# Clustered attention with two MLPs on one core: the centroid similarities with the centroids as stationary operand in four column tiles

## The chip, the core and the metric

The kernel runs on one core of a Trainium2 chip. The metric is the time of one execution on the device, in microseconds (us). The engines are named as the profile names them: PE is TensorE's matmul, PEld its weight load, DVE is VectorE, ACT is ScalarE, POOL is GpSimd, SP is SyncE, which only issues DMAs here.

## What is computed

For 16 heads (2 batches of 8) of 768 tokens by 64 features, each query and key is assigned to the nearest of 16 centroids of its head. A query attends only to keys with the same centroid. The result, laid out as 1536 tokens by 512 features, goes through two MLPs.

```python
q_assign = np.argmax(np.einsum('bhsd,hcd->bhsc', q_n, c_n), axis=-1)
k_assign = np.argmax(np.einsum('bhsd,hcd->bhsc', k_n, c_n), axis=-1)
mask = q_assign[:, :, :, None] == k_assign[:, :, None, :]
scores = scale * np.matmul(q, k.transpose(0, 1, 3, 2))
scores = np.where(mask, scores, -1000000000.0)
...
h = np.maximum(np.maximum(x @ w1, x @ w2), x @ w3)
return (h @ w_out).astype(np.float32)
```

## The kernel before

Two heads make a pair; there are eight pairs, p = 0 to 7, and `qT` and `kT` hold a pair as 128 features by 768 tokens. A unit is 256 queries of one head: 48 units, six to a pair. For a unit the kernel computes scores of 128 queries by 768 keys twice (`scores`, S0 and S1, tile s), the negated row maximum on DVE (`maxima`, M0 and M1, tile mx), the exponential on ACT (`exps`, X0 and X1, tile ee), transposes of it on PE by an identity (`transposes`, T0, T2 and T4, four matmuls each, tile t), copies out of PSUM split into two rounded parts eh and el (E on ACT, L on DVE or POOL), and products with the values (`values`, V0, V2 and V4, four matmuls each, tile o). The mask is carried by extra rows of the score operands: rows 64 to 79 of q2 are the query's one-hot centroid, those of k2 hold 0 or a large negative number.

The order of everything in the attention is written out by hand. `ORDER` has six strings, one for each unit of a pair; "S0/-2" stands for S0 of the unit two ahead, "G0+2" for the operation on the pair two ahead. Each engine executes its part of this list in the list's order. One walk through the six strings is called a turn here, and its strings units 0 to 5. `BEGIN` and `END` hold the first and last operations; the sims of pairs 0 and 1 stand in `BEGIN`.

The change touches the way from a pair's raw operands to the one-hot rows, all of it for a pair that is scored later:

- G0 and G1 (`sims`, line 417): six matmuls each, with 128 tokens of q (G0) or k (G1) as weights and the pair's 32 centroid columns `cb` (block-diagonal over the two heads) as moving operand. They write the spare 256 columns of a score tile, beside its 768 columns of scores.
- N0a, N0b, N1a, N1b (`near_max`, `near_eq`, lines 429 and 435): on DVE, the maximum over the 16 centroids and the equality with it, for q and for k.
- W, FA, FB (lines 447 to 472): the first of equal maxima is kept; the one-hot tile oh of 128 tokens by 6 x 64 comes out in bf16.
- O0 and O1 (`onehot_T`, line 474): three transposes each of 128 tokens by 64 one-hot columns, bf16, into 64 rows of PSUM, again in a score tile's spare columns.
- P0 and P1 (`penalties`, line 492): ACT scales and shifts 64 x 384 of them into the tile oo.
- D0 and D1 (`operands`, line 500): SP issues the DMAs that put the operands together, among them two of 16 x 768 from oo for each head.

G0 stands in unit 2, G1 in unit 3, O0 and P0 in unit 0, O1 and P1 in unit 1. PSUM has eight banks: two score tiles of two banks each (pool `ps_s`), three of one bank for the transposes (pool `ps_t`, tag t) and one for o. A buffer of `ps_t` is given to the next tile that asks for one as soon as the last reader of its old tile stands in the list, and the new writer waits for that reader.

Of the kernel before, what the change touches and what calls it, by code (L numbers as in the profile page):

```python
# [8 lines left out]
F32 = mybir.dt.float32  # L9
F32R = mybir.dt.float32r  # L10
BF16 = mybir.dt.bfloat16
AF = mybir.ActivationFunctionType
ALU = mybir.AluOpType
AX = mybir.AxisListType
# [3 lines left out]
P = 128  # L18
B, H, S, D = 2, 8, 768, 64
C = 16  # L20
NP = H // 2
NPAIR = B * NP
NQ = S // P
G = 256
# [10 lines left out]
SCALE = 0.125  # L35
BIG = 2.0**100
ORDER = (
# [25 lines left out]
)  # L63

ONCE = {
# [10 lines left out]
ENGINE = {"QH": "A", "QH@1": "P", "KH": "P", "VH": "P", "KL": "P", "KL@0": "D", "VL": "P", "W": "P", "W@1": "D"}  # L76
WARM = (8, 4)
PACE = 0.16
FIRST = ("G0", "G1", "N0a", "N0b", "N1a", "N1b", "W", "QH", "KH", "QL", "LD")
SPARE = {"G0": (4, 0), "G1": (5, 0), "O0": (2, 0), "O1": (3, 0)}  # L80
WP = 512

W_LEAST = 2.0 ** ((896 >> 3) - 127)
# [4 lines left out]
def clustered_attention_mlps(  # L88
# [16 lines left out]
    nc = tc.nc  # L105
    PSUM = bass.MemoryType.PSUM

    const = ctx.enter_context(tc.tile_pool(name="const", bufs=1))
# [104 lines left out]
    mlp, m = ctx.enter_context(ExitStack()), {}  # L213
# [104 lines left out]
    with ExitStack() as att:  # L318
# [8 lines left out]
        sm = pool(att, "sm", 2, side="right")  # L327
        ps_t = pool(att, "ps_t", 3, PSUM, "right")
# [10 lines left out]
        idf = const.tile([P, P], F32, name="idf")  # L339
        idb = const.tile([P, P], BF16, name="idb")  # L340
        desc = const.tile([P, C], F32, name="desc")
        gain = const.tile([D + C, 1], F32, name="gain")
        base = const.tile([D + C, 1], F32, name="base")
        cb = const.tile([P, NP, 2 * C], F32, name="cb")


# [2 lines left out]
        st = {}  # L349
# [50 lines left out]
        def split_v(p, part):  # L400
            s = st[p]
            if part == 0:

                s["vs"] = vp.tile([P, NQ, 4, D], F32R, tag="vs", name=f"vs{p}")
            hi, lo = s["vs"][:, :, 0:4:3, :], s["vs"][:, :, 1:3, :]
            if part == 0:
                rounded(engine("VH", p), hi, s["rv"])
            else:
                rest(engine("VL", p), lo, s["rv"], hi)
# [74 lines left out]
        def onehot_up(p, j, ps):  # L484
            ps = ps.bitcast(BF16)[0 : D + C, 0:S]
            for t in range(NQ):
# [2 lines left out]
                    ps[:, t * P : (t + 1) * P], st[p]["oh"][:, c - C : c + D], idb  # L489
                )  # L490

        def penalties(p, half, spare, engine="A"):
            ps = spare.bitcast(BF16)[0 : 4 * C, 0 : S // 2]
            oo = st[p]["oo"][:, half * S // 2 : (half + 1) * S // 2]
            if engine == "A":
                nc.scalar.activation(oo, ps, AF.Identity, scale=gain[0 : 4 * C], bias=base[0 : 4 * C])  # L496
            else:
                nc.vector.tensor_scalar(oo, ps, gain[0 : 4 * C], base[0 : 4 * C], op0=ALU.mult, op1=ALU.add)

        def operands(p, part, heads=(0, 1), queue=nc.sync):  # L500
            s = st[p]

            def dma(out, in_):
                queue.dma_start(out=out.bitcast(F32), in_=in_.bitcast(F32))

            for j in heads:
                r = slice(j * D, (j + 1) * D)
                if part == 0:
                    q1 = opn.tile([P, S], F32R, tag="q1", name=f"q1_{p}_{j}")
                    q2 = opn.tile([D + C, S], F32R, tag="q2", name=f"q2_{p}_{j}")  # L510
                    k1 = opn.tile([P, S], F32R, tag="k1", name=f"k1_{p}_{j}")
                    k2 = opn.tile([D + C, S], F32R, tag="k2", name=f"k2_{p}_{j}")
                    s[j] = (q1, q2, k1, k2)
                    dma(q1[0:D], s["qh"][r])
                    dma(q2[0:D], s["qh"][r])
                    dma(k1[0:D], s["kh"][r])
                    dma(k1[D:P], s["kh"][r])
                    dma(q1[D:P], s["ql"][r])
                else:
                    q1, q2, k1, k2 = s[j]  # L520
                    if part != 2:
                        dma(k2[0:D], s["kl"][r])
                    if part != 1:
                        dma(q2[D : D + C], s["oo"][j * C : (j + 1) * C])
                        dma(k2[D : D + C], s["oo"][(2 + j) * C : (3 + j) * C])

# [177 lines left out]
        def spare(p, op, ahead):  # L704

            if p < ahead:
                return scrap((op, p) if p == 0 else p)[:, 256 * p * int(op[1]) :]
            r, i = SPARE[op]
            return un[(p - ahead) * 2 * NG + r]["spare", i]
# [11 lines left out]
        def do(op, at):  # L721

            o, d = op[:-1], op[-1]
            d = int(d) if d.isdigit() else 0
            if op == "LD":
                load_pair(at)
            elif op == "QH":
                round_q(at)
            elif op == "KH":
                round_k(at)  # L730
            elif op == "QL":
                rest_q(at)
            elif op == "KL":
                rest_k(at)
            elif op == "VH":
                split_v(at, 0)
            elif op == "VL":
                split_v(at, 1)
            elif o == "G":
                sims(at, d, spare(at, op, 2))  # L740
            elif op[0] == "N":
                j = int(op[1])
                if op[2] == "a":
                    near_max(at, j, spare(at, f"G{j}", 2))
                else:
                    near_eq(at, j)
            elif op == "W":
                weigh(at, nc.gpsimd if engine("W", at) == "P" else nc.vector)
            elif op == "FA":
                first_max(at)  # L750
            elif op == "FB":
                first_eq(at)
            elif o == "O":
                onehot_T(at, d, spare(at, op, 1))
            elif op == "SP":
                spread(at)
            elif o == "P":
                penalties(at, d, spare(at, f"O{d}", 1))
            elif o == "D":
                operands(at, 3 * d)  # L760
            elif o == "S":
                scores(at, d)
            elif o in ("SA", "SB"):
                scores(at, d, ("AB".index(o[1]),))
            elif o == "M":
                maxima(at, d)
            elif o == "X":
                exps(at, d)
            elif op == "RA":
                guard(at)  # L770
            elif op == "RC":
                inverse(at)
            elif op == "RB":
                if unit(at)[1] == 1:
                    widen(at)
            elif o == "T":
                transposes(at, d)
            elif o == "E1":
                out_of_psum(at, d, "copy" if way(at, d) == "P" else "hi")
            elif o == "E2":  # L780
                if way(at, d) == "A":
                    out_of_psum(at, d, "copy")
            elif o == "B":
                if way(at, d) == "P":
                    his(at, d)
            elif o == "L":
                rests(at, d)
            elif o == "V":
                values(at, d)
            elif op == "Y":  # L790
                move(at)
            elif op == "K1":
                keep(at)
            elif op == "K2":
                scale(at)
            else:
                raise ValueError(op)

        pieces, scraps = {}, {}
        if True:  # L800
# [28 lines left out]
            nc.vector.memset(base[0 : 2 * C], 0.0)  # L829
            nc.vector.memset(base[2 * C : 4 * C], -BIG)  # L830
            nc.vector.memset(base[D : D + C], -BIG)
            for c in range(C):
                nc.vector.memset(desc[:, c : c + 1], float(C - c))
            nc.vector.tensor_tensor(cn[:, 0, :], ct, ct, op=ALU.mult)
# [178 lines left out]
```

## Time and profile before

| | us |
|---|---|
| median of 3 runs (lowest to highest) | 707.48 (707.19 to 708.02) |
| span of the profiled execution, first to last instruction | 705.9 |
| PE busy in it | 699.4 |
| DVE, ACT, POOL busy | 527.0, 379.6, 285.3 |

The profiled execution is given by its span; the median of the runs lies 1.6 us above it, which is what a run takes around the first and the last instruction. The attention fills about the first 255 us of the span, the MLPs the rest. Matmuls are pipelined and their ends are modelled, so that rows on PE overlap and the distance from one start to the next tells more than a duration. The TensorE clock was granted in full throughout (1.000).

### The profile page before, as it was taken

The numbers are of one execution on the slowest core, as the hardware profiler recorded it, in microseconds if no ns is written. First come the engines' busy times: TensorE is split into PE (matmuls) and PEld (weight loads), VectorE is DVE, ScalarE is ACT, GpSimd is POOL, SyncE is SP. The second block draws the span as 40 slices with busy tenths as digits, with TensorE's granted clock in tenths as the row PEclk, the third lists the DMA queues.
The fourth block names the chain that finished last, engine by engine and source line by source line (L and its number), as shares of the span: only waits on it lengthen the run. The fifth ranks groups of instructions, "written<-read, shape, count | busy, mean of one in ns | idle before, by whom it ended". The sixth has DMA issues, their size and how long they took to land.

```text
span 705.9 us, 10794 instructions
## 1 busy us (share of the span) xinstructions
PE 699.4 (99%) x3876; PEld 601.4 (85%) x3878; DVE 527.0 (75%) x1008; ACT 379.6 (54%) x725; POOL 285.3 (40%) x263
## 2 busy tenths in 40 slices
PE   9999999999999999999999999999999999999997
PEld 6899999999999888888888888888888888888886
DVE  7888998988998788888884599788439846983222
ACT  6888989988999845322321234455434333431220
POOL 3778888888896611101110101333312233221220
PEclk9999999999999999999999999999999999999999
DMA  3887465384460017645553145245405522600112
GB/s 115 217 255 185 98 202 149 83 236 104 125 160 3 1 41 242 208 165 155 176 165 101 52 156 180 90 130 203 144 16 193 179 91 70 197 32 0 46 45 90
DMA packets 29189, 90.00 MB, mean 127 GB/s; under 512 B 4336, under 2 KB 4336, under 8 KB 29136
## 3 DMA queue, kind: packets, MB, share of 16 engines
q1 hardware_dynamic: 28704, 88.13, 41.7%
q10 hardware_dynamic: 432, 1.18, 0.6%
q8 instruction: 31, 0.51, 0.3%
q14 instruction: 22, 0.18, 0.1%
HBM read 68.16 MB, written 3.15 MB: 101 GB/s over the span
## 4 chain that ended last, share of the span: by engine, by line
PE 97%; ACT 2%; DVE 0%; issue 0%; ACTq 0%
PE h L247 13%; PE h L245 13%; PE h L246 13%; PE o L663 9%; PE s L569 9%; PE t L618 9%; PE y L247 8%; PE y L246 8%; PE y L245 8%; PE s L421 2%; PE warm L815 1%; PE o L672 1%; ACT ee L581 1%; PE scrap L421 1%; PE s L479 1%
## 5 line engine op out<-in xcount | busy, mean ns | idle before, releaser
L279 POOL TENSOR_TENSOR hl<-a,hh 128x512 fp32r<-128x512 f32 x66 | 91.8, 1390 | 344.3 <-ACT hh L278 344.3
L245 PE MATMUL h<-xh,wh 128*128 128x512 f32 x408 | 159.1, 390 | 0.0
L246 PE MATMUL h<-xl,wh 128*128 128x512 f32 x408 | 158.9, 390 | 0.1
L247 PE MATMUL h<-xh,wl 128*128 128x512 f32 x408 | 158.8, 389 | 0.0
L278 ACT CAST hh<-a 128x512 fp32r<-128x512 f32 x66 | 41.1, 622 | 124.9 <-DVE a L272 73.8
L245 PE MATMUL y<-hh,wh 128*128 128x512 f32 x264 | 102.7, 389 | 0.0
L246 PE MATMUL y<-hl,wh 128*128 128x512 f32 x264 | 102.7, 389 | 0.0
L247 PE MATMUL y<-hh,wl 128*128 128x512 f32 x264 | 102.7, 389 | 0.0
L575 DVE TENSOR_REDUCE mx<-s 128x1 f32<-128x768 f32 x96 | 91.2, 951 | 15.0 <-PE s L421 10.8
L650 POOL TENSOR_TENSOR el<-et,eh 128x512 fp32r<-128x512 f32 x72 | 99.2, 1386 | 3.0 <-ACT et L635 0.2
L246 PEld LDWEIGHTS h<-xl,wh 128*128 128x128 f32 x408 | 76.6, 188 | 16.7 <-DVE xl L236 0.8
L569 PE MATMUL s<-k,q 128*128 128x512 f32 (+3 forms) x384 | 89.1, 354 | 1.1 <-ACT oo L496 0.8
L247 PEld LDWEIGHTS h<-xh,wl 128*128 128x128 f32 x408 | 76.6, 188 | 15.8
L245 PEld LDWEIGHTS h<-xh,wh 128*128 128x128 f32 x408 | 76.6, 188 | 15.7
L270 ACT COPY a<-h 128x512 f32<-128x512 f32 x66 | 38.6, 585 | 93.3 <-PE h L247 91.7
L581 ACT ACTIVATE ee<-s,mx 128x768 f32<-128x768 f32 x96 | 86.9, 906 | 3.0 <-DVE mx L575 2.1
L274 DVE SCALAR_TENSOR_TENSOR a<-a,h 128x512 f32<-128x512 f32 x48 | 32.9, 684 | 61.8 <-ACT a L270 61.6
L618 PE MATMUL t<-idf,ee 128*128 128x128 f32 x576 | 78.3, 274 | 0.4 <-DVE el L647 0.4
L305 DVE TENSOR_TENSOR acc<-y,acc 128x512 f32<-128x512 f32 x72 | 48.6, 686 | 40.2 <-PE y L247 40.2
L663 PE MATMUL o<-eh,vs 128*128 128x256 f32 x288 | 73.3, 288 | 0.0
L663 PE MATMUL o<-el,vs 128*128 128x256 f32 x288 | 71.8, 282 | 0.0
L618 PEld LDWEIGHTS t<-idf,ee 128*128 128x128 f32 x576 | 65.4, 142 | 2.7 <-DVE el L647 0.6
(103 smaller groups left out, 1153.2 us busy)
## 6 DMA issues: line engine op xcount, KB each, us to landing
raw<-in_w SPq DMA_DIRECT2D x56, 512.0 KB, 3.9
low<-in_w SPq DMA_DIRECT2D x56, 511.5 KB, 3.6
q<-qh SPq DMA_DIRECT2D x28, 192.0 KB, 3.3
k<-kh SPq DMA_DIRECT2D x28, 192.0 KB, 3.7
out_T<-acc SPq DMA_DIRECT2D x12, 256.0 KB, 2.0
rq<-in_qT SPq DMA_DIRECT2D x7, 384.0 KB, 3.9
rk<-in_kT SPq DMA_DIRECT2D x7, 384.0 KB, 5.8
rv<-in_v SPq DMA_DIRECT2D x7, 384.0 KB, 3.6
```

Source lines behind the costliest of these rows:

```text
L245: nc.tensor.matmul(ps, ah, bh, start=(k == 0), stop=False)
L246: nc.tensor.matmul(ps, ah, bl, start=False, stop=False)
L247: nc.tensor.matmul(ps, al, bh, start=False, stop=(k == n - 1))
L278: nc.scalar.copy(hh[:, f, :], a)
L279: nc.gpsimd.tensor_tensor(hlo[:, f, :], a, hh[:, f, :].bitcast(F32), op=ALU.subtract)
L305: nc.vector.tensor_tensor(a, ps, a, op=ALU.add)
L569: nc.tensor.matmul(ps[:, lo:hi], a[:, c0 : c0 + P], b[:, lo:hi], start=start, stop=not start)
L575: nc.vector.tensor_reduce(mx, un[n]["s", i], axis=AX.X, op=ALU.max, negate=True)
L581: nc.scalar.activation(e, u.pop(("s", i)), AF.Exp, bias=u.pop(("m", i)), scale=1.0, accum_out=u["sum"][:, i, 0:1],)
L618: nc.tensor.transpose(ps[:, kk, i * P : (i + 1) * P], u["e"][i][:, (k + kk) * P : (k + kk + 1) * P], idf,)
L650: nc.gpsimd.tensor_tensor(lo, et, hi.bitcast(F32), op=ALU.subtract)
L663: nc.tensor.matmul(u["o"], vs[:, t, :], u[e][:, t, :], start=(t == 0 and e == "eh"), stop=(t == NQ - 1 and e == "el"),)
```

## The change

From pair 2 on, G0 and G1 become one step G (`sims_T`). The 32 centroid columns are now the weights, and 384 tokens of q or k are the moving operand. Four matmuls write four blocks of 32 rows of one PSUM tile g of 128 x 384: q's first and second half, k's first and second half. C (`sims_out`) copies g to SBUF on ACT, H (`sims_back`) transposes it back in three 128 x 128 pieces on PE, and Na and Nb (`all_max`, `all_eq`) do the maximum and the equality for q and k at once. O (`all_onehot_T`) transposes the one-hots in three pieces of 128 columns, P (`all_penalties`) is one activation of 128 x 384, and oo holds 384 columns, so that each head's DMAs from oo become four of 16 x 384. The tiles g and near take buffers of `ps_t`. Pairs 0 and 1 keep the old steps.

```diff
-    "T0/0 E24/1 M1/-1 Y/2 S0/-2 X1/-1 L2/1 E10/0 O0+1 T2/0 T4/0 E12/0 K1/2 RC/1 "
-    "L4/1 S1/-2 K2/2 M0/-2 X0/-2 V0/1 P0+1 RB/1 V2/1 L0/0 E14/0 QL+1 B2/0 V4/1 SP/1 L2/0",
-    "M1/-1 Y/2 B4/1 X1/-1 T0/0 S0/-2 E10/0 K1/2 RA/1 K2/2 O1+1 M0/-2 T2/0 L4/1 T4/0 KL+1 "
-    "S1/-2 E12/0 X0/-2 V0/1 D0+1 P1+1",
+    "T0/0 E24/1 M1/-1 Y/2 S0/-2 X1/-1 L2/1 E10/0 O+1 T2/0 T4/0 E12/0 K1/2 RC/1 "
+    "L4/1 S1/-2 K2/2 M0/-2 X0/-2 V0/1 P+1 RB/1 V2/1 L0/0 E14/0 QL+1 B2/0 V4/1 SP/1 L2/0",
+    "M1/-1 Y/2 B4/1 X1/-1 T0/0 S0/-2 E10/0 K1/2 RA/1 K2/2 M0/-2 T2/0 L4/1 T4/0 KL+1 "
+    "S1/-2 E12/0 X0/-2 V0/1 D0+1",
     "E14/1 L0/1 V2/2 RC/2 V4/2 T0/0 Y/2 RA/0 L2/1 B4/1 E10/0 S0/-2 M1/-1 X1/-1 K1/2 VH+1 "
-    "G0+2 M0/-2 T2/0 E12/0 T4/0 L4/1 V0/1 L0/0 X0/-2 B2/0 L2/0 V2/1 S1/-2 N0a+2 E14/0 "
-    "E24/0 N0b+2 V4/1 RA/1",
-    "T0/0 M1/-1 T2/0 Y/2 S0/-2 E10/0 RC/1 X1/-1 G1+2 E12/0 L4/1 RA/0 K1/2 T4/0 V0/1 VL+1 "
+    "G+2 M0/-2 T2/0 C+2 E12/0 T4/0 L4/1 V0/1 L0/0 X0/-2 B2/0 L2/0 V2/1 H+2 S1/-2 Na+2 E14/0 "
+    "E24/0 Nb+2 V4/1 RA/1",
+    "T0/0 M1/-1 T2/0 Y/2 S0/-2 E10/0 RC/1 X1/-1 E12/0 L4/1 RA/0 K1/2 T4/0 V0/1 VL+1 "
     "RC/0 S1/-2 RC/2 V2/1 E14/0 B4/0 L0/0 V4/1 M0/-2 L2/0 T0/-1 RB/0 D1+1 X0/-2",
-    "QH+2 Y/2 E10/0 M1/-1 N1a+2 T2/0 X1/-1 L4/1 T4/0 RA/0 N1b+2 K1/2 E12/0 S0/-2 RC/0 "
+    "QH+2 Y/2 E10/0 M1/-1 T2/0 X1/-1 L4/1 T4/0 RA/0 K1/2 E12/0 S0/-2 RC/0 "
...
+        def blocks(p):
+            for b in range(4):
+                yield slice(b * 2 * C, (b + 1) * 2 * C), st[p][("rq", "rk")[b // 2]], b % 2 * HALF
+        def sims_T(p):
+            s = st[p]
+            s["g"] = ps_t.tile([P, 2 * G], F32, tag="t", name=f"g{p}")[:, 0:HALF]
+            for rows, r, c in blocks(p):
+                nc.tensor.matmul(
+                    s["g"][rows], cb[:, p % NP, :], r[:, c : c + HALF], start=True, stop=True
+                )
+        def sims_out(p):
...
+            nc.scalar.copy(s["e"].rearrange("p t j h c -> p (t j h c)"), s.pop("g"))
+        def sims_back(p):
...
+            for t in range(NQ // 2):
+                c = slice(t * P, (t + 1) * P)
+                nc.tensor.transpose(s["near"][:, c], e[:, c], idf)
...
+        def all_onehot_T(p, spare):
+            oh = st[p]["oh"][:, D:].rearrange("p (t x) -> p t x", t=NQ // 2)
+            ps = spare.bitcast(BF16)[:, 0:HALF]
+            for t in range(NQ // 2):
+                nc.tensor.transpose(ps[:, t * P : (t + 1) * P], oh[:, t, :], idb)
...
+            nc.scalar.activation(
+                oo, spare.bitcast(BF16)[:, 0:HALF], AF.Identity, scale=gain2, bias=base2
+            )
...
+                    if part != 1 and p >= 2:
+                        for b in range(4):
+                            rows = slice((2 * b + j) * C, (2 * b + j + 1) * C)
+                            cols = slice(b % 2 * HALF, (b % 2 + 1) * HALF)
+                            dma((q2, k2)[b // 2][D : D + C, cols], s["oo"][rows])
...
+            nc.gpsimd.memset(gain2[0:D], 1.0)
+            nc.gpsimd.memset(gain2[D:P], BIG)
+            nc.gpsimd.memset(base2[0:D], 0.0)
+            nc.gpsimd.memset(base2[D:P], -BIG)
```

How this moves instructions shows at three places. The first is PE in unit 2, from the end of S0 to the next S (the numbers behind the names are tile numbers). Before:

```order
L569 MATMUL s_492<-k_0_1_224,q_0_1_222 128x256
L421 MATMUL s_492<-cb,rq_382 128x32 [waits DMAHW1_49]
L421 MATMUL s_492<-cb,rq_382 128x32 x5
L618 MATMUL t_2_514<-idf,ee_0_373 128x128 [waits DVE_49]
...
L618 MATMUL t_4_521<-idf,ee_0_373 128x128 [waits Activation_49]
...
L663 MATMUL o_527<-eh_392,vs_326 128x256 [waits DVE_49]
...
L569 MATMUL s_541<-k_0_1_223,q_0_1_221 128x512 [waits Activation_49]
```

And with the change:

```order
L627 MATMUL s_495<-k_0_1_227,q_0_1_225 128x256
L503 MATMUL g_507<-rq_385,cb 32x384 [waits DMAHW1_49,DVE_49]
L503 MATMUL g_507<-rq_385,cb 32x384
L503 MATMUL g_507<-rk_387,cb 32x384 [waits DMAHW2_49]
L503 MATMUL g_507<-rk_387,cb 32x384
L676 MATMUL t_2_514<-idf,ee_0_376 128x128 [waits Activation_49]
...
L676 MATMUL t_4_524<-idf,ee_0_376 128x128 [waits Activation_49]
...
L519 MATMUL near_544<-idf,e_520 128x128 [waits DVE_49]
L519 MATMUL near_544<-idf,e_520 128x128 x2
L627 MATMUL s_548<-k_0_1_226,q_0_1_224 128x512
```

Six matmuls of 32 moving columns become four of 384, three transposes stand before the next S, and k's share of the sims, which stood in unit 3, is gone from there. The second place is ACT in the same unit: C (line 511) stands between X1 and the copy of T2.

```order
L639 ACTIVATE ee_1_502,sums_110<-s_438,mx_1_500 128x768 [waits DVE_49]
L511 COPY e_520<-g_507 128x384 [waits PE_49]
L693 COPY et_2_522<-t_2_514 128x512 [waits PE_49]
L639 ACTIVATE ee_0_536,sums_107<-s_495,mx_0_512 128x768 [waits DVE_49]
L693 CAST eh_482<-t_4_524 128x512 [waits PE_49]
```

T4's tile takes the buffer that g leaves when C has read it, so T4 now waits for C. The third place is SP, where D1 puts the mask rows of pair 2's first head into its operands:

```order
L557 DMA k_2_0_919<-kl_901 64x768 [waits DMAHW5_49,Pool_49]
L557 DMA q_2_0_917<-oo_840 16x384 [waits DMAHW6_49,Activation_49]
L557 DMA q_2_0_917<-oo_840 16x384 [waits DMAHW7_49]
L557 DMA k_2_0_919<-oo_840 16x384 [waits DMAHW0_49]
L557 DMA k_2_0_919<-oo_840 16x384 [waits DMAHW1_49]
```

There were two issues from oo at this place, each of 16 x 768; now there are four, and the second head's follow in the same way.

## Rows read from the trace of the kernel before

**Rows 1.** The page, part 1: busy us (share of the span) x instructions.

```profile
PE 699.4 (99%) x3876; PEld 601.4 (85%) x3878; DVE 527.0 (75%) x1008; ACT 379.6 (54%) x725; POOL 285.3 (40%) x263
```

**Rows 2.** Windows: one turn; us, PE, PEld, DVE, ACT, POOL busy (x), PEclk, DMA, GB/s.

```profile
116.07:145.07 29.00, 29.00 (x230) 27.37 (x229) 26.81 (x55) 26.43 (x56) 25.14 (x25) 1.00 0.52 130
```

**Rows 3.** Timeline, PE, S0 and transposes alone: start, us, line, tiles, shape, count.

```profile
101.51 0.95 PE L569 MATMUL s<-k,q 128*128 128x512 f32 x4
102.30 1.04 PE L618 MATMUL t<-idf,ee 128*128 128x128 f32 x8
103.09 0.48 PE L569 MATMUL s<-k,q 128*128 128x512 f32 x1
```

**Rows 4.** Timeline, PE, unit 2 with G0 between S0 and the transposes.

```profile
144.28 0.95 PE L569 MATMUL s<-k,q 128*128 128x512 f32 x4
145.07 1.42 PE L421 MATMUL s<-cb,rq 128*128 128x32 f32 x12
...
147.16 0.37 PE L663 MATMUL o<-eh,vs 128*128 128x256 f32 x1
```

**Rows 5.** Timeline, PE, unit 0 with O0 between S0 and the transposes.

```profile
134.89 0.95 PE L569 MATMUL s<-k,q 128*128 128x512 f32 x4
135.77 0.35 PE L479 MATMUL s<-idb,oh 128*64 128x128 bf16 x3
...
136.90 0.48 PE L569 MATMUL s<-k,q 128*128 128x512 f32 x1
```

**Rows 6.** Lines 421 and 618 by themselves: ns least/median/most, first and last start.

```profile
L421 PE MATMUL s<-cb,rq x72: 193/276/276, 29.0 to 175.2; 128*128 128x32 f32 x72
...
L618 PE MATMUL t<-idf,ee x576: 270/272/330, 17.8 to 243.0; 128*128 128x128 f32 x192
```

**Rows 7.** Timeline, PE, near the start: bf16 matmuls on all 128 columns, then transposes.

```profile
21.06 1.04 PE L815 MATMUL warm<-nought 128*128 128x512 bf16 x4
21.94 0.60 PE L618 MATMUL t<-idf,ee 128*128 128x128 f32 x4
```

**Rows 8.** Timeline, PEld, at O0 of rows 5; in brackets idle time before and releaser.

```profile
135.76 0.19 PEld L479 LDWEIGHTS <-oh 128*64 128x64 bf16 x3 [0.25 <-issue]
```

**Rows 9.** Timeline, PE and ACT: four transposes and the copy that waited for them.

```profile
123.20 0.63 PE L618 MATMUL t<-idf,ee 128*128 128x128 f32 x4
...
123.92 0.59 ACT L635 COPY et<-t 128x512 f32<-128x512 f32 x1 [0.30 <-PE t L618]
```

**Rows 10.** Groups by form, 40 to 186 us, ACT: count, busy, mean ns, idle before.

```profile
L635 ACT COPY et<-t 128x512 f32<-128x512 f32 x45 | 26.4, 587 | 7.2 <-PE t L618 7.2
...
L496 ACT ACTIVATE oo<-s,base,gain 64x384 fp32r<-64x384 bf16 x10 | 6.6, 660 | 0.0
```

**Rows 11.** Groups by form, the same stretch, DVE.

```profile
L575 DVE TENSOR_REDUCE mx<-s 128x1 f32<-128x768 f32 x60 | 57.1, 951 | 9.1 <-PE s L421 8.2
```

**Rows 12.** Timeline, SP, the end of D1; and DMA issues: KB, us to landing.

```profile
147.63 0.59 SPq L504 DMA_DIRECT2D k<-oo  x1
...
k<-oo SPq DMA_DIRECT2D x15, 48.0 KB, 2.3
```

**Rows 13.** Timeline, PE, starts of S0: unit 3 with G1, then units 2, 3 without.

```profile
150.16 0.47 PE L569 MATMUL s<-k,q 128*128 128x512 f32 x1
...
156.04 0.47 PE L569 MATMUL s<-k,q 128*128 128x512 f32 x1
...
202.30 0.95 PE L569 MATMUL s<-k,q 128*128 128x512 f32 x4
...
206.89 0.94 PE L569 MATMUL s<-k,q 128*128 128x512 f32 x4
...
211.86 0.47 PE L569 MATMUL s<-k,q 128*128 128x512 f32 x1
```

**Rows 14.** Timeline, POOL, the start of the program.

```profile
3.20 0.56 POOL L836 TENSOR_TENSOR sq<-sq,half 128x1 f32<-128x1 f32 x1 [1.87 <-DVE sq L835]
```

**Rows 15.** Waits from 202 to 213 us: who <- whom: us, times, longest.

```profile
PEld s L569 <- ACT ee L581: 0.3, 1, 0.3
```

More of the change, by code (lines that the diff above doesn't have):

```diff
@@ L78 @@
 PACE = 0.16
-FIRST = ("G0", "G1", "N0a", "N0b", "N1a", "N1b", "W", "QH", "KH", "QL", "LD")
-SPARE = {"G0": (4, 0), "G1": (5, 0), "O0": (2, 0), "O1": (3, 0)}
+FIRST = ("G", "C", "H", "Na", "Nb", "O", "P", "W", "FA", "FB", "QH", "KH", "QL", "LD")
+SPARE = {"O": (2, 0), "O0": (2, 0), "O1": (3, 0)}
+HALF = S // 2
 WP = 512
@@ L341, in clustered_attention_mlps @@
         desc = const.tile([P, C], F32, name="desc")
-        gain = const.tile([D + C, 1], F32, name="gain")
-        base = const.tile([D + C, 1], F32, name="base")
+        lines = const.tile([P, 4], F32, name="lines")
+        gain, base, gain2, base2 = (lines[:, i : i + 1] for i in range(4))
         cb = const.tile([P, NP, 2 * C], F32, name="cb")
@@ L490, in onehot_up, with all_max, all_eq, all_penalties @@
                 )
+        def blocks(p):
[9 more added lines that the diff above has]
+        def sims_out(p):
+            s = st[p]
+            s["m"] = sm.tile([P, NQ, 2, 2, 1], F32, tag="m1", name=f"m1_{p}")
+            s["e"] = sm.tile([P, NQ, 2, 2, C], F32, tag="e", name=f"e{p}", bufs=1)
+            nc.scalar.copy(s["e"].rearrange("p t j h c -> p (t j h c)"), s.pop("g"))
+        def sims_back(p):
+            s = st[p]
+            e = s["e"].rearrange("p t j h c -> p (t j h c)")
+            s["near"] = ps_t.tile([P, 2 * G], F32, tag="t", name=f"near{p}")[:, 0:HALF]
+            for t in range(NQ // 2):
+                c = slice(t * P, (t + 1) * P)
+                nc.tensor.transpose(s["near"][:, c], e[:, c], idf)
+        def all_max(p):
+            ps = st[p]["near"].rearrange("p (n c) -> p n c", c=C)
+            m = st[p]["m"].rearrange("p t j h c -> p (t j h) c")
+            nc.vector.tensor_reduce(m, ps, axis=AX.X, op=ALU.max)
+        def all_eq(p):
+            ps = st[p].pop("near").rearrange("p (n c) -> p n c", c=C)
+            m = st[p]["m"].rearrange("p t j h c -> p (t j h) c")
+            e = st[p]["e"].rearrange("p t j h c -> p (t j h) c")
+            nc.vector.tensor_tensor(e, ps, m.to_broadcast(list(e.shape)), op=ALU.is_equal)
+        def all_onehot_T(p, spare):
[3 more added lines that the diff above has]
+                nc.tensor.transpose(ps[:, t * P : (t + 1) * P], oh[:, t, :], idb)
+        def all_penalties(p, spare):
+            oo = sm.tile([P, HALF], F32R, tag="oo", name=f"oo{p}", bufs=1)
+            st[p]["oo"] = oo
+            nc.scalar.activation(
+                oo, spare.bitcast(BF16)[:, 0:HALF], AF.Identity, scale=gain2, bias=base2
+            )
         def penalties(p, half, spare, engine="A"):
@@ L522, in operands @@
                         dma(k2[0:D], s["kl"][r])
-                    if part != 1:
+                    if part != 1 and p >= 2:
[3 more added lines that the diff above has]
+                            dma((q2, k2)[b // 2][D : D + C, cols], s["oo"][rows])
+                    elif part != 1:
                         dma(q2[D : D + C], s["oo"][j * C : (j + 1) * C])
@@ L738, in do @@
                 split_v(at, 1)
+            elif op == "G":
+                sims_T(at)
+            elif op == "C":
+                sims_out(at)
+            elif op == "H":
+                sims_back(at)
+            elif op == "Na":
+                all_max(at)
+            elif op == "Nb":
+                all_eq(at)
+            elif op == "O":
+                all_onehot_T(at, spare(at, op, 1))
+            elif op == "P":
+                all_penalties(at, spare(at, "O", 1))
             elif o == "G":
```

1 row of the table ONCE is left out of this document.

## The prediction, made before the changed kernel was run

> **What bounds the kernel now.** The page's first part comes first: PE is busy for 99% of the span [rows 1]. That is a busy share of a pipelined engine, so the second view is a window over one turn of the hand-written order: 29.00 us, with PE busy throughout and DVE and ACT at 26.81 and 26.43 [rows 2]. The third is the timeline of PE, for what one inserted step moves. Where nothing stands between S0 and eight transposes, the next score matmul starts 1.58 us after S0 (103.09 less 101.51) [rows 3]. With G0 between them what follows starts 2.88 us after S0 (147.16 less 144.28), so one G costs PE 1.30 us [rows 4]. With O0 it is 2.01 us (136.90 less 134.89), so one O costs 0.43 us [rows 5]. Both lie on the path: PE is the bound in the attention, and what is taken from PE there shortens the kernel as long as DVE, ACT and the waits between them keep up. The MLPs are untouched. The sum is made against the span of 705.9 us; the median of 707.48 us lies 1.6 us above it, and I add the difference to the median.
>
> **What is removed, per turn.** Two G and two O: 2 x 1.30 + 2 x 0.43 = 3.46 us. The sims of pairs 2 to 7 are concerned (72 records for q [rows 6], two for each of six matmuls of six pairs), so there are six such turns, 20.8 us in all.
>
> **What is added, per turn.**
>
> *G's matmuls.* G0 is written as six matmuls and makes twelve records [rows 4]: this form runs two weight loads and two matmuls. Eight transposes in this type take 1.04 us with a last one of 0.27, so one starts every 0.11 us for 128 columns [rows 3, 6]. A record of 384 columns then takes 0.33 us. The form itself agrees: its least duration is 193 ns at 32 columns, against 270 at 128, 0.80 ns a column [rows 6]. In G0 the 32 columns were not what set the pace, the twelve loads of 128-column weights were, at about 0.11 us. Now the weights are small and the moving side is long: eight records of 0.33 us, 2.64 us if they follow each other. No row before shows two matmuls at once in different column blocks. The bounds are 0.66 us (all four blocks at once, two records each) and 3.8 us (no pipelining even between records: 0.27 us + 256 x 0.80 ns = 0.475 us, eight times). I take a value between: blocks do run beside each other, but PE starts matmuls in program order, and the second record of a block needs the same block as the first. Then only the second record of one block runs beside the first of the next: five slots, 1.65 us.
>
> The Trainium skill, "TensorE: Matmul & The Clock Gate", section "Part 3: Packing small matmuls — row/col tiling", says that matmuls in different column groups run concurrently and that three of them gained 2.38 times; it also says that matmuls start and end strictly in program order. By the first half alone G's matmuls would be near the 0.66 us bound; by both they are at the five slots. No run here shows either yet.
>
> *Entering and leaving narrow columns.* O's three records stream 128 columns each. Four bf16 matmuls of 512 columns take 0.88 us to the next start, 0.22 each and no gap behind them [rows 7], so O's three would take 3 x 0.055 = 0.17 us. They cost 0.43, and PEld idles 0.25 us in front of them with nothing named as cause [rows 8]. What differs is the 64 columns. So switching to fewer columns and back costs about 0.27 us; I charge it to G once, with bounds 0 and 0.54, and not to the new O, which is 128 wide.
>
> *H and O.* H is three transposes of 0.11 us, 0.33 us. O is three of between 0.055 us (its columns) and 0.11 us (its weights at the rate above); I take 0.2 us for the three.
>
> *The new wait of T4.* T4's buffer comes free when C has read g. C can start about 0.09 us after the modelled end of G's last matmul, as the copy at 123.92 us did after transposes that end at 123.83 [rows 9]. It copies 384 columns, and 512 take 0.59 us, so 0.44 in proportion and 0.59 at most [rows 10]; I take 0.5. T2's four transposes hide 0.44 us of that. I charge 0.2 us; bounds 0 and 0.6, the latter if an exponential still stands in front of C on ACT. Behind T4 on PE are V0, V2, H and S1, which all shift with it.
>
> *Other engines.* ACT trades two activations of 0.66 us for one and C of about 0.5 [rows 10]: nothing lost. DVE does the same elements in two operations instead of four, and M0 need no longer wait for sims in its own bank, which cost DVE 8.2 us in five turns [rows 11]; neither is on the path while PE bounds. On SP four more issues of 0.59 us a turn, 2.4 us, stand at the end of D1: without them the last ends at 148.22 us and lands 2.3 us later [rows 12], with them at about 153; S0 of that head comes no earlier than 156.04 us [rows 13]. So I cost them at nothing; were that slack gone, S0 would wait up to 2.4 us a turn. The four new memsets on POOL fall into its idle 1.87 us before line 836 [rows 14].
>
> *What the others give back.* In the turn after the last G0 there are no sims. Its unit 2 takes 4.59 us (206.89 less 202.30) and its unit 3 takes 4.97 (211.86 less 206.89), where unit 3 with G1 took 5.88 (156.04 less 150.16) [rows 13]. So the whole 1.30 is got in unit 2, but only 0.91 in unit 3: there S1 waits 0.3 us for an exponential [rows 15]. In the changed kernel unit 2 stays long and lets ACT catch up, so I charge half of the missing 0.38 us, 0.19.
>
> Sum per turn: -3.46 + 1.65 + 0.27 + 0.33 + 0.2 + 0.2 + 0.19 = -0.62 us; six turns, -3.7 us: **703.8 us**. With the friction at 0.38 and T4's wait at 0.4 it is -0.23 a turn (706.1); with no switching cost and no friction -1.08 (701.0).
>
> **Rivals.**
>
> *The blocks run one after the other.* G's matmuls take 2.64 us, unit 2 grows so long that the friction goes, and the sum is -3.46 + 2.64 + 0.27 + 0.33 + 0.2 + 0.2 = +0.18 us a turn, +1.1 us: 708.6, and up to 710.8 us with T4's wait at 0.6. The point from which it decides is a record of about 0.31 us (2.46 / 8). For it: nothing before shows blocks side by side, and the two records of a matmul follow each other. This is also the case in which the change doesn't do what it says.
>
> *All four blocks at once.* 0.66 us, and C then finds ACT busier: T4's wait at 0.4 and friction at about 0.65, since DVE's 26.81 us leave little below a turn of 27.5 us [rows 2]. -3.46 + 0.66 + 0.27 + 0.33 + 0.2 + 0.4 + 0.65 = -0.95 to, without the last term, -1.6 us a turn; I take -1.15, -7 us: 700.5. Against it: order on one block.
>
> *Each block drains the array.* The 0.25 us stall in front of O [rows 8] could be paid at each change of block. Then G takes about 3.8 us and the sum is about +1.34 us a turn, +8 us: 715.5. It decides from one drain of about 0.1 us between records on. Against it: the three records of O, all in one block, follow without gaps, which says nothing of a change of block.
>
> **How the numbers follow.** Overlap of neighbours 0.42, one after the other 0.28, all at once 0.20, drains 0.10. About 0.2%, 1.4 us, is what a measurement of this kernel can tell from no change. The first case is faster nearly throughout (0.40), the third wholly (0.20), the second gives 0.03 to faster, 0.13 to the same and 0.12 to slower, the first 0.02 to the same, the fourth 0.10 to slower: 0.63, 0.15, 0.22. The range from 699.5 to 711.0 holds the first two cases and 0.12 of the third, 0.82. The likeliest case's own range is 701.0 to 706.1.
>
> **What would show it.** In the new profile, G's eight records should span about 1.65 us plus the last one's end, with the starts of records 2 and 3, 4 and 5, 6 and 7 close together; eight starts 0.33 us apart mean the first rival. O's three records should follow S0 without an idle 0.25 us on PEld, and G's first weights should have it. A turn should take 28.4 us instead of 29.00, with unit 2 longer (4.59 + 1.65 + 0.27 + 0.33 + 0.2, about 7.0 us from S0 to S0) and unit 3 near 4.6 to 5.0. T4 should wait for C by some tenths, and no S for a DMA from oo. The prediction is wrong if a turn is not shorter by 0.2 us or more, or if PE idles in units 0 or 1.

## The result, and the profile after

| | before | after |
|---|---|---|
| median us of the runs (lowest to highest) | 707.48 (707.19 to 708.02) | 712.00 (711.36 to 714.04) |
| span of the profiled execution, us | 705.9 | 709.6 |

The changed kernel is slower: the ratio is 1.0069, with a 95% interval of 1.0054 to 1.0083, some 4.5 us where 3.7 us of gain were forecast. The page's busy times and, below them, its chain of work that ended last, by engine:

```profile
PE 695.0 (98%) x3780; PEld 588.0 (83%) x3782; DVE 534.0 (75%) x996; ACT 378.9 (53%) x725; POOL 286.7 (40%) x267
...
PE 81%; DVE 10%; ACT 4%; issue 2%; POOL 2%; DMA 0%; ACTq 0%; DVEq 0%; POOLq 0%
```

Against [rows 1], PE lost 4.4 us of work and DVE gained 7.0 us, though the change took 12 instructions from DVE. The chain before was:

```profile
PE 97%; ACT 2%; DVE 0%; issue 0%; ACTq 0%
```

PE stood at 97% there; now DVE has a tenth of the chain. So PE was relieved, as meant, and for part of the time something on DVE holds the kernel up in its place. A window over one turn, the counterpart of [rows 2], in the same columns:

```profile
98.23:128.16 29.93, 28.37 (x216) 25.13 (x213) 28.63 (x53) 26.25 (x56) 25.07 (x25) 1.00 0.60 164
```

The turn is 0.93 us longer, PE is busy for 28.37 us of it instead of throughout, and DVE is at 28.63. What got longer on DVE shows in its groups by form from 68 to 158 us (count, busy, mean ns), after and then before; L168 and L177 were L166 and L175:

```profile
L168 DVE SCALAR_TENSOR_TENSOR wx<-raw,wt 128x512 uint32<-128x512 uint32 x3 | 4.5, 1508 | 0.0
...
L177 DVE TENSOR_TENSOR wl<-low,wt 128x512 fp32r<-128x512 f32 x2 | 3.7, 1872 | 0.0
```

```profile
L166 DVE SCALAR_TENSOR_TENSOR wx<-raw,wt 128x512 uint32<-128x512 uint32 x3 | 2.4, 790 | 0.0
...
L175 DVE TENSOR_TENSOR wl<-low,wt 128x512 fp32r<-128x512 f32 x2 | 1.5, 762 | 0.0
```

These lines are in no part of the diff and in no term of the prediction. They belong to `Weights.piece`, which splits the first MLP's weights into wh and wl from the words as loaded, 512 columns at a time. A third hand-written table, `ONCE`, spreads it over the attention: an entry `(8, 20): "w00"` does the next step of piece 0 in unit 8 of 48, ahead of item 20 of that unit's string. A step is one DVE operation of 128 x 512 from SBUF to SBUF; there are 28, five in each of turns 1 to 5 (unit 1, twice unit 2, units 3 and 4) and three in turn 6. Together they took 15.6 us before and 26.0 us after. The timeline of after shows why. First DVE, then POOL, each with start and duration:

```profile
117.50 0.94 DVE L633 TENSOR_REDUCE mx<-s 128x1 f32<-128x768 f32 x1
118.36 1.58 DVE L168 SCALAR_TENSOR_TENSOR wx<-raw,wt 128x512 uint32<-128x512 uint32 x1
...
120.79 0.55 DVE L524 TENSOR_REDUCE m<-near 128x24 f32<-128x384 f32 x1
121.45 0.56 DVE L530 TENSOR_TENSOR e<-near,m 128x384 f32<-128x384 f32 x1
...
123.44 2.17 DVE L177 TENSOR_TENSOR wl<-low,wt 128x512 fp32r<-128x512 f32 x1
```

```profile
118.11 1.28 POOL L708 TENSOR_TENSOR el<-et,eh 128x512 fp32r<-128x512 f32 x1
...
123.23 1.83 POOL L380 TENSOR_TENSOR vs<-rv,vs 128x768 fp32r<-128x768 f32 x1
```

POOL begins at 118.11 and 123.23; the step comes 0.25 and 0.21 us later, and ends 0.55 us after POOL's operation both times (119.94 against 119.39, 125.61 against 125.06). In the kernel before it is the other way round; DVE, then POOL:

```profile
122.11 0.84 DVE L175 TENSOR_TENSOR wl<-low,wt 128x512 fp32r<-128x512 f32 x1
```

```profile
122.37 2.29 POOL L378 TENSOR_TENSOR vs<-rv,vs 128x768 fp32r<-128x768 f32 x1
```

The step comes 0.26 us ahead of POOL, takes 0.84 us, and POOL takes 2.29 in place of 1.83. POOL has slack and DVE has little, so it matters who begins.

Why the order turned can be read too, though from the timelines alone; no run tests it by itself. Na and Nb stand ahead of unit 3's step and take 0.55 + 0.56 us where N0a and N0b took 0.35 + 0.36: 0.40 us more, and the lead was 0.26. Counted from S0 of unit 2, the step now begins at 7.17 us instead of 6.83, and POOL's operation at 6.96 instead of 7.09. In unit 2, M0 began 2.25 us after S0 before (117.53 less 115.28), since it waited for G0 in its own bank [rows 11], and now begins 1.23 us after it (117.50 less 116.27). So DVE now reaches the step 0.25 us after POOL has begun L4's subtraction. Before, that subtraction was over, at 118.10 us, when the step began; DVE, then POOL, of before:

```profile
117.53 0.96 DVE L575 TENSOR_REDUCE mx<-s 128x1 f32<-128x768 f32 x1 [1.33 <-PE s L421]
118.40 0.68 DVE L166 SCALAR_TENSOR_TENSOR wx<-raw,wt 128x512 uint32<-128x512 uint32 x1
```

```profile
116.83 1.27 POOL L650 TENSOR_TENSOR el<-et,eh 128x512 fp32r<-128x512 f32 x1
```

The waits of after from 68 to 158 us show who pays (total us, times, longest):

```profile
ACT ee L639 <- DVE mx L633: 9.6, 10, 2.0
PEld t L676 <- DVE el L705: 3.2, 7, 0.6
PEld o L721 <- DVE acc L746: 2.8, 3, 0.9
```

The maxima and the evictions queue behind a long step, the exponentials and then PE wait for them. Before, in the longer stretch from 40 to 186 us, the first of these waits was small, and the list of waits of PE's matmuls is empty:

```profile
ACT ee L581 <- DVE mx L575: 1.6, 6, 0.3
```

### The profile page after: what moved, and what is told of

The parts are those of the page before. It is cut to its first block, busy times and chain, and to the rows that moved or that the text cites. A ratio compares the mean times of both kernels' runs of the same rounds, so it can differ in the third digit from the quotient of the medians.

```text
span 709.6 us, 10635 instructions
## 1 busy us (share of the span) xinstructions
PE 695.0 (98%) x3780; PEld 588.0 (83%) x3782; DVE 534.0 (75%) x996; ACT 378.9 (53%) x725; POOL 286.7 (40%) x267
## 4 chain that ended last, share of the span: by engine, by line
PE 81%; DVE 10%; ACT 4%; issue 2%; POOL 2%; DMA 0%; ACTq 0%; DVEq 0%; POOLq 0%
PE h L248 13%; PE h L249 13%; PE h L247 13%; PE y L248 8%; PE y L247 8%; PE y L249 8%; PE o L721 5%; PE t L676 5%; PE s L627 4%; DVE mx L633 3%; DVE el L705 2%; ACT ee L639 1%; POOL el L708 1%; PE warm L887 1%; DVE wl L177 1%
## 5 line engine op out<-in xcount | busy, mean ns | idle before, releaser
L627 PE MATMUL s<-k,q 128*128 128x512 f32 (+3 forms) x384 | 90.6, 358 | 2.1 <-ACT oo L549 0.8
L676 PE MATMUL t<-idf,ee 128*128 128x128 f32 x576 | 80.0, 275 | 3.0 <-DVE el L705 2.2
```

The costliest lines, as they stand in the source:

```text
L627: nc.tensor.matmul(ps[:, lo:hi], a[:, c0 : c0 + P], b[:, lo:hi], start=start, stop=not start)
L676: nc.tensor.transpose(ps[:, kk, i * P : (i + 1) * P], u["e"][i][:, (k + kk) * P : (k + kk + 1) * P], idf,)
```

## The experiments

A turn is measured here from the first score matmul of unit 6k to that of unit 6k+6 (a stall late in a turn shows in the next one). Turns 1 to 6, in us, from the profiled execution of each kernel, and the median time:

| kernel | turns 1 to 6 | sum | time |
|---|---|---|---|
| before | 29.00 29.04 29.00 29.01 29.00 26.82 | 171.9 | 707.48 |
| after | 27.69 29.91 29.92 29.65 29.06 27.32 | 173.6 | 712.00 |
| late_before | 29.00 29.01 29.00 29.01 29.00 26.42 | 171.4 | (725.4) |
| late_after | 27.21 27.21 27.21 27.21 27.21 25.73 | 161.8 | (715.7) |
| before_stuck | 29.27 29.84 29.83 29.79 29.26 27.26 | 175.2 | 711.22 |
| o1_back | 27.74 29.94 29.95 29.69 29.07 27.42 | 173.8 | 709.81 |
| restored | 27.73 29.65 29.67 29.40 28.81 27.36 | 172.6 | 707.65 |
| vl_later | 27.25 28.84 28.31 28.58 28.33 27.39 | 168.7 | 703.69 |
| gaps_a | 28.12 29.08 29.10 28.81 28.82 27.13 | 171.1 | 705.93 |
| gaps_b | 27.21 28.06 27.92 28.32 28.57 27.10 | 167.2 | 701.74 |
| gaps_c | 27.20 27.98 27.45 27.74 27.47 26.25 | 164.1 | 700.97 |

The turns come from one profiled execution of each kernel. The two kernels called late were run once; their times, in brackets, hold all steps in one piece behind the turns, so that only their turns are compared.

**The steps taken out of the turns, in both kernels.** The same edit of `ONCE` in each; the loads of weights f02 to f11 go along with the steps:

```diff
-    (4, 11): "f00", (5, 2): "f01", (7, 12): "w00", (8, 20): "w00", (8, 29): "w00", (9, 20): "w00",
...
-    (46, 0): "in", (46, 12): "x0", (46, 15): "x1", (46, 19): "x2", (47, 1): "x3", (47, 2): "ph h h",
+    (4, 11): "f00", (5, 2): "f01",
+    (46, 0): "w00 w00 w00 w00 w00 w00 w00 f02 w01 w01 w01 w01 w01 w01 w01 f03 w02 ... f11 in",
+    (46, 12): "x0", (46, 15): "x1", (46, 19): "x2", (47, 1): "x3", (47, 2): "ph h h",
```

On late_after:

> The changed kernel with its 28 weight-split steps taken out of turns 1 to 6 and done in one piece at the start of unit 46 (so the end of the attention gets about 12 to 18 us longer, and the total says nothing; the turns are read, from the first score matmul of unit 6k to that of unit 6k+6). Theory 1 (the steps on VectorE are stretched behind GpSimd operations and hold up the eviction of transposes and maxima): turns 2 to 5 fall from 29.9, 29.9, 29.7, 29.1 to 27.4 to 28.0 us each. Theory 2 (the new order itself makes T4 wait for C, and piles H, Na and Nb into unit 2): they stay at 29.3 us or more.

On late_before:

> The same move in the kernel before, as a control. Theory 1: TensorE set its turns, so turns 2 to 5 stay at 28.9 to 29.0 us though VectorE is relieved of about 3 us a turn. If they fall below 28.5, the steps cost time in the old kernel too, and the drop in the other run has to be read against this one.

One turn of late_after and one of late_before, in the columns of [rows 2]:

```profile
95.12:122.33 27.21, 27.20 (x215) 25.00 (x214) 23.80 (x47) 25.51 (x54) 23.70 (x25) 1.00 0.53 137
```

```profile
98.30:127.30 29.00, 29.00 (x232) 27.37 (x230) 24.54 (x50) 25.59 (x54) 23.63 (x25) 1.00 0.51 129
```

Without the steps the changed kernel's turn is 27.21 us five times over, slightly below the range expected, with PE busy throughout; the old kernel's stays at 29.00. So the change by itself is worth 1.79 us a turn, 9.6 us over turns 1 to 6, and PE bounds again. The steps cost the old kernel 0.4 us in these turns (171.9 less 171.4) and the changed one 11.8 (173.6 less 161.8). Theory 2, that the new order of C, H, Na and Nb costs the time, falls. It is in these turns that the terms of the prediction can be measured; PE's timeline of late_after at G and at O:

```profile
111.67 0.94 PE L627 MATMUL s<-k,q 128*128 128x512 f32 x4
112.54 0.52 PE L503 MATMUL g<-rq,cb 128*32 128x384 f32 x2
112.55 0.52 PE L503 MATMUL g<-rk,cb 128*32 128x384 f32 x2
112.89 0.49 PE L503 MATMUL g<-rq,cb 128*32 128x384 f32 x2
112.90 0.49 PE L503 MATMUL g<-rk,cb 128*32 128x384 f32 x2
113.32 1.32 PE L676 MATMUL t<-idf,ee 128*128 128x128 f32 x8
...
115.44 0.49 PE L519 MATMUL near<-idf,e 128*128 128x128 f32 x3
115.68 0.95 PE L627 MATMUL s<-k,q 128*128 128x512 f32 x4
```

```profile
102.98 0.95 PE L627 MATMUL s<-k,q 128*128 128x512 f32 x4
103.77 0.34 PE L536 MATMUL s<-idb,oh 128*128 128x128 bf16 x3
103.94 1.04 PE L676 MATMUL t<-idf,ee 128*128 128x128 f32 x8
104.75 0.94 PE L627 MATMUL s<-k,q 128*128 128x512 f32 x4
```

**The stall made in the old kernel.** Before, with unit 3's step moved behind L0 in five turns:

```diff
-(9, 20): "w00", (15, 20): "w01", (21, 20): "w01", (27, 20): "w02", (33, 20): "w03"
+(9, 23): "w00", (15, 23): "w01", (21, 23): "w01", (27, 23): "w02", (33, 23): "w03"
```

> The kernel before with one weight-split step a turn (unit 3, turns 1 to 5) moved behind L0's subtraction on VectorE, so that it comes up after GpSimd has begun its 2 us subtraction for v. Theory 1: the moved step takes 1.4 to 2.2 us in place of 0.4 to 0.85, and the kernel gets 2 to 6 us slower (ratio 1.003 to 1.008). Theory 2: the step takes as long as before and the time stays within 1.4 us.

The time rose to 711.22 us, ratio 1.0049 (1.0034 to 1.0064), and turns 2 to 4 to 29.8 us. DVE and POOL of this kernel, at the place of the two rows of before above:

```profile
124.02 2.04 DVE L175 TENSOR_TENSOR wl<-low,wt 128x512 fp32r<-128x512 f32 x1
```

```profile
123.68 1.82 POOL L378 TENSOR_TENSOR vs<-rv,vs 128x768 fp32r<-128x768 f32 x1
```

The same operation, 0.34 us behind POOL instead of 0.26 ahead of it, takes 2.04 us instead of 0.84, and again ends 0.56 us after POOL. The five moved steps took 1.67 to 2.04 us. Only the place of these five steps was changed, so it is the order of the two engines that makes the loss. (Two of the five, in turns 1 and 3, take an operation of ACT along; turns 2 and 4, where none does, are as long as turn 3.)

**Entries of `ONCE` that slipped.** Its indices count items of a string, and the change took items out of the strings and put others in. Pair 1's O1, which the change moved into `ONCE`, ended up behind M0 in unit 1, and x0 to x2 of unit 46, which split the first MLP's input, two items later. First O1 alone:

```diff
-    (1, 11): "O1@1",
+    (1, 10): "O1@1",
```

> The changed kernel with pair 1's O1 put back ahead of M0 in unit 1 (one index earlier, as in the kernel before). If the 1.4 us gap of TensorE near 25 us goes and is not given back later: 1.1 us faster than the changed kernel, about 710.9 us (ratio 1.005 to the kernel before). If other engines set the end of turn 0: no change, 712 us.

The time was 709.81 us (ratio 1.0023, 1.0013 to 1.0032), 2.2 us below the changed kernel; its ten runs lie between 707.83 and 710.07 us. Turn 0 explains half of the gain, the 1.1 us expected: 26.81 us instead of 27.96, as the wait shown here in PE's timeline of after went away (O1 writes into the bank that M0 reads):

```profile
26.31 0.33 PE L481 MATMUL s<-idb,oh 128*64 128x128 bf16 x3 [1.09 <-DVE mx L633]
```

The rest lies ahead of turn 0, in code that is the same: the first scores start at 11.90 us here, at 12.67 in after, and between 11.72 and 12.73 in the runs of this study, so I don't count it. Then all slipped entries together:

```diff
-(1, 11): "O1@1", (7, 12): "w00", (8, 20): "w00", (8, 29): "w00", (9, 20): "w00", (10, 20): "w00",
+(1, 10): "O1@1", (7, 11): "w00", (8, 21): "w00", (8, 31): "w00", (9, 19): "w00", (10, 18): "w00",
...
-(46, 12): "x0", (46, 15): "x1", (46, 19): "x2"
+(46, 10): "x0", (46, 13): "x1", (46, 17): "x2"
```

> The changed kernel with every entry of the table ONCE moved back to the neighbours that it had in the kernel before (pair 1's O1 ahead of M0, the weight steps of units 1, 3 and 4, and the splits x0 to x2 of unit 46, which the removed items had shifted by one to three places); the weight steps of units 2 and 3 keep their place on VectorE. Theory 1 (what counts is when a step comes up against GpSimd): the two long steps a turn stay long (1.3 to 2.2 us each), turns 2 to 5 stay at 29.3 to 29.9; gained are 1.1 us in turn 0, about 1.4 us between the last scores and the first MLP, and some tenths a turn: 707 to 709 us. Theory 3 (the slipped entries are the cause): turns near 27.4 us and a time near 697 us.

707.65 us, ratio 0.9998 (0.9989 to 1.0007). From the first score matmul of unit 47 to the end of the span it takes 473.2 us, as before (473.1), where after and o1_back take 474.5 and 474.6: that is x0 to x2. Against o1_back, turns 2 to 5 fell by only 0.26 to 0.29 us, which fits the step of unit 4 that is back in its place (0.42 us instead of 0.67); the two long steps of a turn stay long in turns 1 to 4. Turn 5, at 28.81 us, lies below the range expected, as it did in after (29.06). From after to restored the slips account for about 3.4 us (1.15 in turn 0, 0.94 in turns 1 to 6, 1.28 behind the last scores), and the bulk of the loss in the turns remains. Theory 3 falls as the main cause.

**The GpSimd operation moved instead of the step.** In restored, unit 3:

```diff
-    "T0/0 M1/-1 T2/0 Y/2 S0/-2 E10/0 RC/1 X1/-1 E12/0 L4/1 RA/0 K1/2 T4/0 V0/1 VL+1 "
-    "RC/0 S1/-2 RC/2 V2/1 E14/0 B4/0 L0/0 V4/1 M0/-2 L2/0 T0/-1 RB/0 D1+1 X0/-2",
+    "T0/0 M1/-1 T2/0 Y/2 S0/-2 E10/0 RC/1 X1/-1 E12/0 L4/1 RA/0 K1/2 T4/0 V0/1 "
+    "RC/0 S1/-2 RC/2 V2/1 E14/0 B4/0 VL+1 L0/0 V4/1 M0/-2 L2/0 T0/-1 RB/0 D1+1 X0/-2",
```

> As restored, with nothing moved on VectorE: in unit 3 GpSimd's second pass over v (VL, 1.8 to 2.1 us) stands one GpSimd instruction later, behind B4's copy. Theory 1 (the step is long because GpSimd began first): unit 3's step falls from 1.7 to 2.15 us to 0.4 to 0.7, unit 3 from 5.44 to about 4.6 us, turns from 29.7 to 28.7 to 29.2, 702.5 to 705.5 us. If a step's length depends on the step itself or on the load of VectorE: unit 3's step stays over 1.3 us and the time at 707.6.

703.69 us, ratio 0.9941 (0.9925 to 0.9958). The orders of DVE, ACT and PE are word for word those of restored (the step's index goes down by one with the item taken out ahead of it), and 4.0 us are gained by one POOL instruction a turn that begins after the step instead of before it. DVE, then POOL:

```profile
119.37 0.67 DVE L177 TENSOR_TENSOR wl<-low,wt 128x512 fp32r<-128x512 f32 x1
```

```profile
122.06 1.84 POOL L380 TENSOR_TENSOR vs<-rv,vs 128x768 fp32r<-128x768 f32 x1
```

The step of unit 3 took 0.40 to 0.67 us in all five turns, and unit 3 took 4.58 us instead of 5.44. That B4's copy on POOL comes earlier by this edit can't be the gain: in late_after VL stands ahead of B4 and unit 3 takes 4.59 us. The step of unit 2, which was left, still took 1.3 to 1.6 in all turns but one, and one step of unit 4 (at 68.46 us) took 1.45 us behind a POOL operation that it had not met in restored.

**Steps put where POOL pauses.** Three placements of the steps, with the other entries as in restored (in gaps_c the last two loads of weights, f10 and f11, come four and five units later as well). One turn's entries:

```diff
-(7, 11): "w00", (8, 21): "w00", (8, 31): "w00", (9, 19): "w00", (10, 18): "w00"
+gaps_a: (7, 11): "w00", (8, 28): "w00 w00 w00", (10, 18): "w00"
+gaps_b: (7, 11): "w00", (8, 28): "w00 w00", (10, 16): "w00", (10, 18): "w00"
+gaps_c: (7, 11): "w00", (8, 28): "w00 w00", (10, 18): "w00"
```

> As restored, but three of the five weight steps a turn stand together in unit 2 behind L0's subtraction, where VectorE idles for 1.8 us in the run without weight steps, one in unit 1 and one in unit 4 ahead of L2; none is left in unit 3. Theory 1: no step above 1.0 us but perhaps one of the three, turns 1 to 5 of 27.3 to 27.9 us, 697 to 701 us (ratio 0.986 to 0.992), faster than both kernels. If VectorE's load itself (23.8 us and 2.6 us of steps in a turn of 27.2) is too high whatever the places: turns of 28.5 us or more, 704 us or more.

> As gaps_a with two steps together in unit 2 and two in unit 4 (ahead of M0 and ahead of L2). Theory 1: no step above 1.0 us, turns 1 to 5 of 27.3 to 27.9 us, 697 to 701 us; should the step ahead of M0 delay the scores of the next unit, some tenths a turn more than gaps_a.

> As gaps_b without the step ahead of M0 in unit 4: four steps a turn (one in unit 1, two in unit 2, one in unit 4 ahead of L2) in turns 1 to 6, the last four in units 43 and 44. Theory 1, with what gaps_b showed (its turns of 28.1 us against 27.2 in the run without steps; the step ahead of M0 holds up the maxima, the exponentials and the next scores): turns 27.4 to 27.8 us, 699 to 701 us. If the remaining 0.9 us came from the pair of steps in unit 2: no change to gaps_b, 701.7 us.

gaps_a was a miss: 705.93 us (ratio 0.9974, 0.9963 to 0.9984) and turns of 28.1 to 29.1. The third step of the three met POOL's next subtraction and took 1.40 to 1.67 us in five turns, a stall at a new place. Its time would fit the other theory on record too, that DVE's load is too high whatever the places; but gaps_b, with as many steps in a turn, is 4.2 us faster, so the load alone is not the cause. gaps_b has no step above 1.0 us; it ran in 701.74 us (0.9919, 0.9905 to 0.9932), just above the 697 to 701 expected, and four of its turns are 27.9 to 28.6 us, where 27.3 to 27.9 were expected. gaps_c, without the step ahead of M0, came within the time expected (turns 1 and 2, at 27.20 and 27.98 us, lie on either side of the range): 700.97 us, ratio 0.9901 (0.9886 to 0.9916), 6.5 us faster than the kernel before and 11 faster than the change as made. A turn of it:

```profile
94.57:122.02 27.45, 27.33 (x215) 25.05 (x214) 25.89 (x51) 26.07 (x54) 24.11 (x25) 1.00 0.66 178
```

PE is busy for all but 0.12 us of it again. gaps_c also has one step fewer in each of turns 1 to 5, and whether the place or the number of the steps won its last 0.8 us over gaps_b was not separated. Its four last steps in units 43 and 44, two of them at 1.1 and 1.4 us, and the last load of weights behind them are the likely cause of some 1.4 us that it loses after the last scores (474.7 us to the end, 473.3 in gaps_b); a better place for them was not tried.

## Why the prediction was wrong

- **The sum was made for PE alone, and the step that failed is "Other engines".** It said of DVE that its fewer operations and M0's earlier start are "neither on the path while PE bounds". It put DVE at nothing by counting its operations, and the sum has no term for the weight steps. PE bounded, but DVE had only 2.2 us of slack in a turn [rows 2], and most of its weight steps began only 0.04 to 0.4 us ahead of a POOL operation. With M0 no longer waiting and with Na and Nb longer, DVE moved against POOL by 1.3 us in unit 2 and by 0.5 us in unit 3, and the steps fell behind POOL's operations. The steps became 10.4 us longer (26.0 less 15.6), and what they cost in turns 1 to 6 rose by 11.3 us (11.76 against 0.43). None of the rivals had this. The chance of 0.22 for slower rested on blocks that run one after the other and on a drain between blocks; the trace of late_after shows neither.
- **Removed, 3.46 us a turn:** right. From before to late_after unit 3 got 1.28 us shorter (5.87 to 4.59) for a G1 put at 1.30, and unit 1 got 0.44 shorter (4.59 to 4.15) for an O1 put at 0.43.
- **G's matmuls and the switch of columns, 1.65 + 0.27:** much too high, the term of PE's part that was mis-sized. In late_after the transposes start 1.65 us after S0 (113.32 less 111.67) where they start 0.79 after it without G [rows 3]: 0.86 us for both. The first records of q's and k's blocks start within 0.02 us, the second ones 0.35 us later: all four blocks at once, the second rival, which had a chance of 0.20. The argument for five slots, program order on one block, falls: the second records of a block start behind the first records of all four. That matmuls in different column groups run concurrently ("TensorE: Matmul & The Clock Gate", section "Part 3: Packing small matmuls — row/col tiling", of the Trainium skill) is what this trace shows too. Its strict order of starts holds here among the first records (q's from 112.54, k's from 112.55 us) and among the second ones (112.89 and 112.90), but it does not put a block's second record ahead of the next block's first, as I took it to.
- **H at 0.33, O at 0.2, T4's wait at 0.2:** 0.24 (115.68 less 115.44), 0.19 (1.77 us from S0 to the next S, less 1.58), and 0.25 by the row below, the waits of late_after over two turns. About right. PEld's idle time in front of O did not go, though: it is 0.16 us in late_after, where 0.25 stood before; in front of G's first weights it is 0.24, as expected.

```profile
PEld t L676 <- ACT e L511: 0.5, 2, 0.2
```

- **Friction at 0.19:** none in unit 3, from which it was read. It came from the weight steps: the unit 3 without sims takes 4.97 us before [rows 13] and 4.58 us in late_before, where the wait for an exponential [rows 15] is gone too. In the unit ahead of it a step began 0.54 us behind POOL's subtraction and took 1.03 us instead of 0.42. So the kind of stall that decided the result stood in the trace of before; DVE, then POOL:

```profile
204.16 1.03 DVE L168 TENSOR_SCALAR wt<-wx 128x512 uint32<-128x512 uint32 x1
```

```profile
203.62 1.28 POOL L650 TENSOR_TENSOR el<-et,eh 128x512 fp32r<-128x512 f32 x1
```

- **PE's part in all:** -3.46 + 0.86 + 0.24 + 0.19 + 0.25 = -1.92 us a turn, measured -1.79; the 0.13 between them is not accounted for. So PE's part went the way forecast, with three times the size. That gaps_c ran close to the 700.5 us of the rival with all blocks at once is luck in part: that rival had -1.15 us a turn, and gaps_c gives some of its -1.79 back to steps and behind the last scores. The first rival's upper end should have been 711.0 us, not 710.8; the range does not change by it.
- **SP and the memsets at nothing:** right as far as it shows; no score matmul of after waits for a transfer from oo, and the first scores start within the spread of equal code.
- **Indices into the strings were not looked at:** `ONCE` refers to items by number. Two slips cost about 1.1 us in turn 0 and 1.3 us at the end.
- **The accounts of the profiled execution** (+3.7 us of span): start 0.6 (spread of equal code), turn 0 nothing (1.1 gained by the first G, 1.1 lost by O1), turns 1 to 6 +1.7 (9.6 gained, 11.3 more for the steps), the last scores nothing, after them 1.4.

## What to carry to other kernels

When PE is relieved by a few per cent in a stage whose other engines stand at over nine tenths, as here in the attention, they can decide the gain: look at every operation that two engines may contend for, and ask on which side of the other engine's operation it will fall after the shift. A long operation from SBUF to SBUF on DVE wants a place where POOL pauses, or one where DVE is there first; moving the POOL operation does as well. Tables that refer to a list by index have to be carried along when the list gets shorter.

## What was not expected of the hardware

In these traces, when a step on DVE and an operation on POOL both work from SBUF to SBUF, the one that begins second finishes late. The steps with two inputs ended 0.55 us behind POOL's operation (1.58 and 2.17 us for operations that take 0.67 to 0.68 alone). Steps with one input ended 0.28 us behind it: the one at 93.78 us in after took 1.91 us, where the same step takes 0.40 in vl_later with POOL idle. So it is the end of POOL's operation that sets a step's length. POOL behind the step took 2.29 us in place of 1.83. The Trainium skill says this under "SBUF — State Buffer", section "Who interferes with whom": operations of DVE with two inputs in SBUF, or in a mode that uses two ports, contend with GpSimd, and issue order decides which of the two fully blocks. The runs agree in both directions (before_stuck and vl_later). A few steps in turns 5 and 6 of several runs don't fit: at 178.21 us in after a step began 0.26 us behind POOL and took 0.41 us, and POOL took 1.81 in place of 1.28. Starts on POOL are rough in these records; whether the step was really second there stays open.

Four float32 matmuls with 32 weight columns each, in the four column blocks, take two records of 384 columns each. The trace of late_after has the four first records within 0.02 us and the four second ones together 0.35 us later, which is near the 0.33 us estimated for one record alone from [rows 3] and [rows 6].
